# Loading later batches in the order of the attention's chunks, and copying v's global rows in two parts

## The chip, the cores and the metric

One core of a Trainium2 chip. The program runs on this core alone. The metric is the device time of one execution in microseconds (us); lower is better. The kernel before: 201.15 us, median of 3 runs (200.98 to 203.73).

A run is called slow if it took over 1.5% more than the fastest run of the same kernel, and comparisons use the other, fast, runs. Where two kernels are compared, a ratio is the mean time of the one's fast runs over that of the other's of the same rounds, so it is not quite the ratio of the medians quoted beside it.

## The reference

A sparse attention is followed by a gated long convolution. With 4 batches, 8 heads, 768 positions and 64 dimensions:

```python
keep = is_global | is_local      # the first 8 keys, and the last 96 up to the query
scores = where(keep, scale * q @ k.T + bias, -1e9)
a = exp(scores - max); a = a / (sum(a) + 1e-9)
x = (a @ v) as [batch, seq, 512]
x1, x2, x3 = split(x @ w_proj)                   # w_proj 512 x 1536
y = x1 * irfft(rfft(x2) * rfft(filter)) * x3     # along the sequence
out = y @ w_out
```

What matters here: every query attends to the first 8 keys. The kernel therefore keeps v in 7 tiles of 128 partitions: 120 rows of the sequence each, and in partitions 0 to 7 of **every** tile the same 8 global rows.

## The kernel before: the parts concerned

The kernel lists its operations with what they read and write; a scheduler written in it orders them for each engine. `load` issues a DMA from GpSimd ("G", casting float32 to float16) or SyncE ("S"):

```python
def load_rows(self, what, dst, src, b, t):        # 120 rows of k or v into one tile
    lo, hi = self.K0[t], self.K0[t] + KL
    self.load("G", dst[P - (hi - lo):P, t, :, 0:self.D], ...)

def load_v(self, b, ts):                          # [cut: reading vt, s]
    if b == 1:
        self.g.op("V", 0.2, lambda _: memset(vt[:, :, :, self.D:], 1.0), w=[("vn1", s)], ...)
    for t in ts:
        self.load_rows(("vn", s), vt, self.v, b, t)
        if t == 0:
            self.load_global(vt, s)

def load_global(self, vt, s):                     # the global rows: one copy, SBUF to SBUF
    self.load("S", vt[0:NG], vt[NG:2 * NG, 0:1].to_broadcast([NG, 7, self.H, self.D + 1]),
              [("vng", s)], (56, 1040), "vglobal", r=[("vn", s, 0), ("vn1", s)])

def load_batch(self, b):                          # batches 1 to 3
    for t in range(6):
        self.load_q(b, t)
    for t in range(7):
        self.load_rows(("kn",), self.kn, self.k, b, t)
    self.load_v(b, range(7))
```

Tile 0 of v is loaded from row 0 on, so its partitions 8 to 15 hold the global rows; the copy spreads them to partitions 0 to 7 of all tiles. The attention of a batch goes in three chunks, of tiles (0,1), (2,3) and (4,5,6). A chunk's values wait for the copy:

```python
def values(self, hp, c, slot):                    # head pair hp, chunk c
    def run(_):  # [cut] for each head and tile: E of the tile times v of the tile (L743),
                 # then E's overlap times v of the tile before (L748)
    vs = [("vn", slot, t) for t in range(max(0, ts[0] - 1), ts[-1] + 1)] + [("vn1", slot), ("vng", slot)]
    g.op("P", 0.03 * n, run, acq=[b], r=es + vs, name="values")
```

The first batch has a loader of its own, already by thirds, with its loads in the order q, k, v of a chunk.

The softmax here doesn't subtract the row's maximum and nothing guards it: scores larger than these inputs give would overflow.

Of the kernel before, what the change touches and what calls it, by code (L numbers as in the profile page):

```python
# [17 lines left out]
NG = 8  # L18
# [12 lines left out]
def dve(n, rate=1, psum=False):  # L31
    return 0.068 + (0.005 if psum else 0.0) + n / rate / 960.0
# [250 lines left out]
class Fused:  # L283
# [124 lines left out]

    def load_v(self, b, ts):
        vt, s = self.vn[b % 2], b % 2  # L410
        if b == 1:
            self.g.op("V", 0.2, lambda _: self.nc.vector.memset(vt[:, :, :, self.D:], 1.0),
                      w=[("vn1", s)], name="ones")
        for t in ts:
            self.load_rows(("vn", s), vt, self.v, b, t)
            if t == 0:
                self.load_global(vt, s)

    def load_global(self, vt, s):
        self.load("S", vt[0:NG], vt[NG:2 * NG, 0:1].to_broadcast([NG, 7, self.H, self.D + 1]),  # L420
                  [("vng", s)], (56, 1040), "vglobal", r=[("vn", s, 0), ("vn1", s)])

    def load_w(self, o, n):
        wr = self.w_proj.rearrange("(t p) n -> p t n", p=P)
# [302 lines left out]
    def values(self, hp, c, slot):  # L727
        nc, g, D = self.nc, self.g, self.D
        ts = self.GRP[c]
        nt = len(ts)  # L730
        b = g.bank()
        vt, xn = self.vn[slot], self.xn[hp]

        def view():
            return b.f32()[:, 0:2 * nt * (D + 1)].rearrange("p (h t d) -> p h t d", h=2, t=nt)

        def run(_):
            o, first = view(), True
            for hh in range(2):
                ef = self.E[hp][:, hh]  # L740
                for i, t in enumerate(ts):
                    at = 248 * t if t < 6 else 248 * 5 + 168
                    nc.tensor.matmul(o[:, hh, i], ef[:, at:at + P], vt[:, t, 2 * hp + hh, :],  # L743
                                     start=first, stop=(t == 0), skip_group_check=True)
                    first = False
                    if t > 0:
                        at = 248 * (t - 1) + KL
                        nc.tensor.matmul(o[:, hh, i], ef[:, at:at + P],  # L748
                                         vt[:, t - 1, 2 * hp + hh, :], start=False, stop=True,
                                         skip_group_check=True)  # L750
        n = 2 * sum(2 if t else 1 for t in ts)
        es = [("E", hp, i, hh) for i in range(max(0, c - 1), c + 1) for hh in range(2)]
        vs = [("vn", slot, t) for t in range(max(0, ts[0] - 1), ts[-1] + 1)] + [("vn1", slot), ("vng", slot)]
        g.op("P", 0.03 * n, run, acq=[b], r=es + vs, name="values")
        rc = self.rc[self.turn % 4]
        key = ("rc", self.turn % 4)
        self.turn += 1

        def scaled(_):
            o = view()  # L760
            r = rc[:, 0:2 * nt].rearrange("p (h t o) -> p h t o", h=2, o=1)
            nc.vector.reciprocal(r, o[:, :, :, D:D + 1])  # L762
            nc.vector.tensor_mul(xn[:, ts[0]:ts[0] + nt].rearrange("p t h d -> p h t d"),  # L763
                                 o[:, :, :, 0:D], r.to_broadcast([P, 2, nt, D]))
        g.op("V", 0.16 + 0.04 * nt + dve(2 * nt * D, 1, True), scaled, use=[b], w=[("xn", hp, c), key], name="xn")
# [214 lines left out]
                  [("g", 1, j, s) for j in range(4) for s in range(2)], (768, 2048), "filter")  # L980

    def load_batch(self, b):
        for t in range(6):
            self.load_q(b, t)
        for t in range(7):
            self.load_rows(("kn",), self.kn, self.k, b, t)
        self.load_v(b, range(7))

    def graph(self):
        g = self.g  # L990
# [61 lines left out]
```

## Time and profile before

| | before, the profiled run |
|---|---|
| time of that run / span in the profile | 199.61 us / 197.6 us |
| TensorE busy | 185.8 us, 94% |
| TensorE's waits for the copy | 2.0 us (batch 0), 1.9 us (batch 1) |
| mean granted clock of TensorE | 0.991 |

The span is from the first to the last instruction that the profiler saw; a run's time is some 2 us longer. The granted clock is TensorE's share of full speed. A mean of 0.991 over 197.6 us is 1.8 us of lost clock: one drop to half speed for 3.4 us (54.41 to 57.83 us at 0.50). The lines themselves are in the prediction.

### The profile page before, as it was taken

The numbers are of one execution on the slowest core, as the hardware profiler recorded it, in microseconds if no ns is written. First come the engines' busy times: TensorE is split into PE (matmuls) and PEld (weight loads), VectorE is DVE, ScalarE is ACT, GpSimd is POOL, SyncE is SP. The second block draws the span as 40 slices with busy tenths as digits, with TensorE's granted clock in tenths as the row PEclk, the third lists the DMA queues.
The fourth block names the chain that finished last, engine by engine and source line by source line (L and its number), as shares of the span: only waits on it lengthen the run. The fifth ranks groups of instructions, "written<-read, shape, count | busy, mean of one in ns | idle before, by whom it ended". The sixth has DMA issues, their size and how long they took to land.

```text
span 197.6 us, 4679 instructions
## 1 busy us (share of the span) xinstructions
PE 185.8 (94%) x1758; PEld 109.9 (56%) x1758; DVE 151.2 (77%) x383; ACT 155.6 (79%) x337; POOL 75.7 (38%) x96
## 2 busy tenths in 40 slices
PE   7965999999699999999999999999999999999992
PEld 2545767665435467665456756754556675445540
DVE  7795974997749999995099998994598999259630
ACT  7777995969868989994799979865897975785842
POOL 8799972799968918992000500000000000000000
PEclk9999999999969999999999999999999999999999
DMA  6999999999999999999700560005200000214025
GB/s 143 195 164 146 160 202 193 155 151 132 146 157 141 135 101 62 139 138 159 277 2 3 37 41 2 3 2 211 111 0 0 3 0 6 103 53 159 2 109 209
DMA packets 90885, 20.52 MB, mean 104 GB/s; under 512 B 83728, under 2 KB 87792, under 8 KB 90864
## 3 DMA queue, kind: packets, MB, share of 16 engines
q0 software_dynamic: 80912, 12.14, 101.8%
q1 hardware_dynamic: 9952, 8.10, 12.8%
q8 instruction: 13, 0.21, 0.5%
q14 instruction: 8, 0.07, 0.1%
HBM read 25.82 MB, written 6.29 MB: 163 GB/s over the span
## 4 chain that ended last, share of the span: by engine, by line
PE 77%; POOL 6%; DVE 5%; DMA 4%; ACT 3%; issue 2%; POOLq 0%; ACTq 0%; DVEq 0%
PE bank L805 21%; PE bank L852 11%; PE bank L892 10%; PE bank L872 8%; PE bank L645 7%; PE bank L694 5%; PE bank L743 3%; PE bank L778 3%; PE bank L658 3%; DMA vn<-vn 3%; POOL kn L383 3%; PE bank L748 2%; DMA kn<-in_k_dram 2%; POOL vn L383 2%; PE bank L685 2%
## 5 line engine op out<-in xcount | busy, mean ns | idle before, releaser
L709 ACT ACTIVATE E<-bank 128x432 f16<-128x432 f32 x96 | 43.7, 555 | 3.1 <-PE bank L694 2.9
L805 PE MATMUL bank<-xT,w 128*128 128x384 f16 x256 | 44.6, 326 | 0.5 <-DVE xT L367 0.3
L383 POOL DMA_DIRECT2D kn<-in_k_dram x28 | 26.2, 943 | 31.8 <-PE bank L645 18.7
L805 PEld LDWEIGHTS <-w 128*128 128x128 f16 x256 | 24.7, 98 | 17.3 <-issue 1.2
L383 POOL DMA_DIRECT2D vn<-in_v_dram x28 | 25.3, 916 | 0.9 <-DVE qn L367 0.9
L763 DVE TENSOR_TENSOR xn<-bank,rc 128x256 f16<-128x256 f32 (+1 forms) x48 | 22.5, 468 | 1.7
L371 ACT ACTIVATE ot<-bank 128x512 f32<-128x512 f32 x24 | 14.3, 597 | 10.8 <-PE bank L892 10.8
L892 PE MATMUL bank<-wo,y 128*128 128x512 f16 x96 | 22.4, 379 | 0.0
L743 PE MATMUL bank<-vn,E 128*128 128x65 f16 x224 | 17.5, 194 | 4.1 <-DMA kn<-in_k_dram 2.0
L813 DVE TENSOR_TENSOR g<-bank,x 128x384 f16<-128x384 f32 x32 | 17.3, 551 | 4.9 <-PE bank L805 4.5
L743 PEld LDWEIGHTS <-E 128*128 128x128 f16 x224 | 15.1, 98 | 8.8 <-DVE E L722 2.7
L371 ACT ACTIVATE x<-bank 128x384 f16<-128x384 f32 x27 | 13.4, 504 | 7.9 <-PE bank L805 6.5
L645 PE MATMUL bank<-ab,fwd 128*128 128x512 f16 x72 | 18.6, 379 | 0.0
L872 PE MATMUL bank<-inv,X 128*128 128x384 f16 x96 | 18.4, 326 | 0.1
L383 POOL DMA_DIRECT2D qn<-in_q_dram x18 | 16.1, 910 | 3.6 <-PE bank L694 1.7
L748 PE MATMUL bank<-vn,E 128*128 128x65 f16 x192 | 17.1, 194 | 0.0
L367 ACT CAST X<-bank 128x512 f16<-128x512 f32 x23 | 13.8, 603 | 3.0 <-PE bank L645 2.4
L367 ACT CAST eo<-bank 128x384 f16<-128x384 f32 x30 | 14.5, 507 | 2.0 <-PE bank L872 1.7
L762 DVE RECIPROCAL rc<-bank 128x4 f32<-128x4 f32 (+1 forms) x48 | 8.6, 178 | 9.3 <-PE bank L748 4.8
L694 PE MATMUL bank<-QT,KT 64*128 64x216 f16 (+2 forms) x224 | 15.4, 245 | 0.3 <-ACT E L709 0.2
L367 ACT CAST ab<-bank 128x512 f16<-128x512 f32 x20 | 11.9, 607 | 4.4 <-PE bank L852 4.4
L892 PEld LDWEIGHTS <-y 128*128 128x128 f16 x96 | 9.4, 98 | 10.6
(112 smaller groups left out, 344.9 us busy)
## 6 DMA issues: line engine op xcount, KB each, us to landing
out_dram<-ot SPq DMA_DIRECT2D x24, 256.0 KB, 2.0
kn<-in_k_dram POOLq DMA_DIRECT2D x28, 120.0 KB, 5.6
vn<-in_v_dram POOLq DMA_DIRECT2D x28, 120.0 KB, 6.7
qn<-in_q_dram POOLq DMA_DIRECT2D x18, 128.0 KB, 7.9
ot<-in_q_dram SPq DMA_DIRECT2D x6, 256.0 KB, 6.9
w<-in_moe_w_proj_dram POOLq DMA_DIRECT2D x4, 256.0 KB, 7.0
g<-in_moe_filter_fft_dram POOLq DMA_DIRECT2D x1, 768.0 KB, 12.8
w<-in_moe_w_proj_dram POOLq DMA_DIRECT2D x1, 512.0 KB, 9.7
```

What stands on the lines that cost most here:

```text
L367: {"A": nc.scalar.copy, "V": nc.vector.tensor_copy, "G": nc.gpsimd.tensor_copy}[e](out, in_)
L371: self.nc.scalar.mul(out, in_, c)
L383: return self.g.op(eng, 0.57 + 0.00035 * nbytes[0] if eng == "G" else 0.5, lambda _: e.dma_start(dst, src), w=w, r=r, nbytes=nbytes, name= ...
L645: self.nc.tensor.matmul(b.f32(), self.fwd[:, kt, s, :], src[i][:, kt, :], start=(kt == 0), stop=(kt == 2))
L694: nc.tensor.matmul(bs[hh].f32()[:, off:off + w], self.KT[hs, hp, P * m:P * m + P], self.QT[hs, hp, KL * m:KL * m + w], start=(off == 0 and ...
L709: g.op("A", act(432), lambda _, hh=hh: nc.scalar.activation(eo[:, hh], bs[hh].f32()[:, 0:432].rearrange("p (m w) -> p m w", m=2), Act.Exp, ...
L743: nc.tensor.matmul(o[:, hh, i], ef[:, at:at + P], vt[:, t, 2 * hp + hh, :], start=first, stop=(t == 0), skip_group_check=True)
L763: nc.vector.tensor_mul(xn[:, ts[0]:ts[0] + nt].rearrange("p t h d -> p h t d"), o[:, :, :, 0:D], r.to_broadcast([P, 2, nt, D]))
L805: nc.tensor.matmul(bk.f32()[:, 0:h], self.w[:, c, o + P * j:o + P * j + P], self.xT[:, c, h * s:h * s + h], start=(c == 0), stop=(c == 3))
L852: nc.tensor.matmul(bk.f32(), src[:, c, P * t:P * t + P], w[:, c, DM:2 * DM], start=(c == 0), stop=(c == 3))
L872: nc.tensor.matmul(bk.f32()[:, 0:h], X[:, s, cs], self.inv[:, s, :], start=(s == slots[0]), stop=(s == slots[-1]))
L892: nc.tensor.matmul(bk.f32(), y[:, c, P * t:P * t + P], self.wo[:, c, :], start=(c == 0), stop=(c == 3))
```

## The change

Two ideas. **Order**: for a batch after the first, the loads go by thirds (q, k and v of chunk 0, then of chunk 1, and so on), so tile 0 of v comes sixth instead of fourteenth and the copy can go sooner. **Split**: the copy goes in two parts, for tiles 0 and 1 (all that chunk 0 needs) and for the other five.

```diff
     def load_v(self, b, ts):
-        if b == 1:
+        if b == 1 and ts[0] == 0:
...
     def load_global(self, vt, s):
-        self.load("S", vt[0:NG], vt[NG:2 * NG, 0:1].to_broadcast([NG, 7, self.H, self.D + 1]),
-                  [("vng", s)], (56, 1040), "vglobal", r=[("vn", s, 0), ("vn1", s)])
+        for c, (t, n) in enumerate(((0, 2), (2, 5))):
+            self.load("S", vt[0:NG, t:t + n], vt[NG:2 * NG, 0:1].to_broadcast(
+                [NG, n, self.H, self.D + 1]), [("vng", s, c)], (8 * n, 1040), "vglobal",
+                r=[("vn", s, 0), ("vn1", s)])
...
-        vs = [("vn", slot, t) for t in range(max(0, ts[0] - 1), ts[-1] + 1)] + [("vn1", slot), ("vng", slot)]
+        vs = [("vn", slot, t) for t in range(max(0, ts[0] - 1), ts[-1] + 1)] + [("vn1", slot)] + [
+            ("vng", slot, i) for i in range(max(0, c - 1), min(c, 1) + 1)]
...
     def load_batch(self, b):
-        for t in range(6):
-            self.load_q(b, t)
-        for t in range(7):
-            self.load_rows(("kn",), self.kn, self.k, b, t)
-        self.load_v(b, range(7))
+        for c in range(3):
+            for t in ([0, 1, 2], [3, 4], [5])[c]:
+                self.load_q(b, t)
+            for t in self.GRP[c]:
+                self.load_rows(("kn",), self.kn, self.k, b, t)
+            self.load_v(b, self.GRP[c])
```

A comparison of the two built programs: TensorE, VectorE and ScalarE keep their sequence, except for one idle ("filler") matmul more on TensorE. GpSimd's order changes for batch 1 alone, since the scheduler had brought batches 2 and 3 to thirds already. SyncE has four copies more.

## The prediction

> **What bounds the kernel now.** I read the page's shares first, then TensorE's own waits, then the chain that ended last, then GpSimd's timeline around the one wait that the chain shows to be a DMA, and last a table of short windows.
>
> ```profile
> PE 185.8 (94%) x1758; PEld 109.9 (56%) x1758; DVE 151.2 (77%) x383; ACT 155.6 (79%) x337; POOL 75.7 (38%) x96
> ...
> PEclk9999999999969999999999999999999999999999
> DMA  6999999999999999999700560005200000214025
> ```
>
> TensorE is busy 94% of 197.6 us, so all that moving loads about can win is in the 11.8 us of its idle time and in the one slice where its clock digit drops to 6. The DMA row is full until about 100 us and nearly empty later: a change of load order can matter only in the first half.
>
> ```profile
> PE bank L743 <- DMA kn<-in_k_dram: 2.0, 1, 2.0
> PE bank L743 <- DMA vn<-vn: 1.9, 1, 1.9
> PE bank L658 <- DVE qn L367: 1.6, 1, 1.6
> ```
>
> These are TensorE's three longest waits in its own list. Line 743 is the first matmul of the attention's values. It happens twice: at 18.14 us (batch 0) and at 53.31 us (batch 1). Batches 2 and 3 have no such wait.
>
> The first is put down to a load of k, and I don't believe that. The matmul waits on two semaphores: that of the copy of the global rows of v, and that of v's tile 0. In the trace's semaphore records, the k load that the list names lands at 18.21 us or later, after the matmul has started; tile 0 of v had landed by 12.36 us; the copy's semaphore is complete at 18.0 us. So both waits are for the same thing, the copy vn<-vn that spreads 8 rows of tile 0 to all seven tiles.
>
> ```profile
> 46.25 0.86 PE bank L852 x4
> 47.11 0.35 PE bank L519 x6
> 47.46 0.02 issue
> 47.48 0.14 DVE inv L367
> 47.62 5.55 DMA vn<-vn
> 53.18 0.14 issue
> 53.31 0.22 PE bank L743 x2
> ```
>
> In the chain (start, us, what) the batch-1 copy takes 5.55 us from issue to landing, and TensorE is idle for the last 1.92 us of it. It is issued only at 47.62 us because tile 0 of v is the 14th of the batch's 20 loads:
>
> ```profile
> 31.27 0.94 POOL L383 DMA_DIRECT2D kn<-in_k_dram  x1 [1.37 <-DMA w<-in_moe_w_proj_dram]
> 35.09 0.92 POOL L383 DMA_DIRECT2D kn<-in_k_dram  x1 [2.89 <-DMA g<-in_moe_filter_fft_dram]
> 36.28 2.83 POOL L383 DMA_DIRECT2D kn<-in_k_dram  x3 [0.27 <-issue]
> 39.90 1.79 POOL L383 DMA_DIRECT2D kn<-in_k_dram  x2 [0.79 <-PE bank L805]
> 41.68 6.27 POOL L383 DMA_DIRECT2D vn<-in_v_dram  x7
> ```
>
> The seven v loads begin at 41.68 us, and the first lands 5.9 us later (47.56).
>
> ```profile
> 51.40:53.30 1.90, 0.00 (x0) 0.02 (x1) 0.99 (x3) 1.90 (x5) 1.49 (x2) 1.00 1.76 147
> 54.40:57.80 3.40, 3.40 (x23) 1.23 (x21) 1.52 (x6) 1.88 (x4) 1.72 (x3) 0.50 2.26 161
> ```
>
> The windows table (busy PE, PEld, DVE, ACT, POOL, then clock) shows the second cost of that wait: after 1.9 us without a matmul the next 3.4 us run at a clock of 0.50.
>
> [...]The 2.0 us gap at 16.1 to 18.1 us was not followed by a drop.
>
> [...]56 packets of 1040 bytes and 8 late semaphore steps for each copy. The split keeps the 8 partitions, [...]with 2 or 5 rows each instead of 7.
>
> [...]in the first copy (issued 12.44) an engine's seven rows start 0.07 us apart[...], but the engines' first rows start anywhere from 15.29 to about 16.7 us.
>
> **The change part by part.**
>
> *Order of loads.* The program order tells that TensorE, VectorE and ScalarE keep their sequences, banks included, but for one filler matmul. On GpSimd only batch 1 changes; in batches 2 and 3 the order was already q, k, v by thirds, as buffers come free that way. In batch 1 tile 0 of v moves from 14th to 6th.
>
> When is it issued? Each GpSimd load waits for the load eight places earlier, whose semaphore it takes over. q0 to q2 keep 22.84 to 25.86 us. k0 then follows the second weight load (landed 25.77), k1 the third (27.15), v0 the fourth (28.48), v1 the fifth (30.98). Next comes q3, behind the filter (34.80). So v0 is issued at about 28.5 instead of 41.68 us. Seven loads are outstanding behind the filter in either kernel when it lands, and v0 is the sixth of them: it lands where q5 landed, at about 40.0 us. The copy follows at once, and even at the old 5.55 us it is in place by 45.6 us, nearly 6 us before it is wanted at 51.4. What pays for it is q3, q4, k2 and k3: they land at about 41.8 to 44.3 us, and are wanted at 49.6 and 50.8. So nothing new should wait.
>
> How much of the 1.92 us comes back? The masked E of head pairs 0 and 1 is done by VectorE at about 51.0 and 51.5 us, that of pair 2 at 52.4, with one 0.65 us transform between. So the first values can start at about 51.4, and 1.8 of the 1.92 us is won.
>
> *The clock drop.* 3.41 us at half speed cost 0.5 x 3.41 = 1.7 us wherever TensorE is the bound, and in 54.6 to 57.8 it is: VectorE waits 1.81 us and ScalarE 1.40 us for it. In the profiled run this would also go. [...]I take half: 0.85 us.
>
> *Passing it on.* From 59.4 us VectorE is full and carries the chain. It idled 1.30 + 1.81 + 0.82 = 3.9 us between 52.4 and 59.4, all for TensorE, so it can start up to that much earlier. I let 95% through. After 86 us TensorE is at 100% and the shift is carried to the end.
>
> *Copy in two parts.* Five rows fewer in each engine at 0.07 us are 0.35 us off the first part, out of 5.55[...]. So at batch 0 I expect the wait to fall from 2.04 to about 1.7 us only. The added filler (about 0.22 us at the idle matmul's spacing) stands between pairs 2 and 3 of these very values and takes most of that back. Net 0.1 us. The four added issues are on SyncE, which idles; the 5-row part lands well before chunk 1 asks for it (22.2 us).
>
> Sum: 1.8 + 0.85 + 0.1 = 2.75, times 0.95 = 2.6 us; I add 0.2[...]: 2.8 us. 201.15 - 2.8 = about 198.3 us.
>
> **The rivals.**
>
> *The wait is replaced.* If the values were really held by E or by a bank, removing the copy would show a VectorE or ScalarE wait in its place and win under 1 us: about 200.5. Against it: ScalarE was busy through the gap, but on later work, and VectorE's masks for pairs 0 and 1 were finished by 51.54.
>
> *The loads that were pushed back hold TensorE.* q3, q4, k2 and k3 have 6 to 8 us in hand by the estimate above. If GpSimd were held longer behind the filter, TensorE would wait at line 658 instead, and the time would be 200 to 202. The filter landed at 34.8 us and 11 loads at 0.9 us follow; I see no room for that.
>
> *The split wins all of the batch-0 wait as well.* If queueing behind casting loads scales with rows[...], the first part takes 5.55 x 2/7 plus some 2 us and the wait of 2.04 goes. Then 2 us more are won, and with a clock drop avoided in some runs the time is 195.5 to 196.5. The packets of 0.07 us in bursts speak against it, though the batch-1 copy shows rows taking 0.14 us on average.
>
> *Nothing reaches the end*, because VectorE's stretch from 60 to 85 us absorbs it: about 200.5. Its idle time before 59.4 us speaks against it.
>
> **Range and chances.** The central case has 1.8 us sure and 0 to 1.7 us from the clock: 197.5 to 199.3. Rival three[...] reach down to 196.3, the first two up to 200.2. Faster by over 2% needs 4.0 us, which needs the clock drop in every run before and a piece of the third rival: 0.17. Slower has no cause that I can see but the filler and DMA luck: 0.02.
>
> **What would show it.** In TensorE's waits after: the 1.9 us on vn<-vn is gone; the 2.0 us at line 743's first matmul (line 745 now), whatever load it is put down to, is still 1.4 to 2 us. GpSimd issues v0 of batch 1 at 28 to 30 us and its copy goes out at about 40. The clock is 1.00 from 50 to 60 us. The values of batch 1 start at about 51.3, and the gate matmuls that began at 69.10 begin 2 to 3.5 us earlier. A wait for qn or kn at line 660 near 49 us, or a batch-0 wait under 1 us, would prove me wrong.

## The result, and the profile after

The changed kernel: **195.93 us** median (194.91 to 198.54, 4 runs); before, in the same rounds, 201.06 (200.55 to 203.73, 4 runs). Ratio of fast runs 0.9741, 95% interval 0.9685 to 0.9796: faster by 2.6%. The prediction of 198.3 us was 2.4 us too high, and the result lies just below its range, which began at 196.3.

The profile taken with this result fell in the slowest of the four runs (198.54 us). Its clock row and its longest wait on TensorE (columns: what waits, its releaser, then us in total, times, longest us):

```profile
PEclk9999699999999999999999999999999999999999
```

```profile
PE bank L745 <- DMA vn<-vn: 1.8, 1, 1.8
```

The drop in this run is at 20 us, in batch 0, and the only copy that TensorE still waits for is batch 0's. For a comparison with the profile of before I use a later profile of the same changed kernel (e4 below: 195.5 us, span 194.0 us), a fast run. Its page: shares, clock and DMA.

```profile
PE 184.9 (95%) x1759; PEld 109.8 (57%) x1759; DVE 150.7 (78%) x383; ACT 155.0 (80%) x337; POOL 76.0 (39%) x96
...
PEclk9999999999999999999999999999999999999999
DMA  6999999999999999999500900015100001114035
```

TensorE is busy 0.9 us less than before on one matmul more; nothing ran at half clock. TensorE's waits of the same run:

```profile
PE bank L745 <- DMA kn<-in_k_dram: 1.6, 1, 1.6
PE bank L660 <- DVE qn L367: 1.5, 1, 1.5
PE bank L363 <- DVE idle L434: 1.2, 1, 1.2
```

One wait at the first values is left, that of batch 0 (again put down to a load of k; the semaphore records show the copy). Next come lines of GpSimd's timeline and of TensorE's (start, us, engine, line, operation, count), then the two windows in which before had 0.00 us of matmul and a clock of 0.50 (start:end, length, then busy PE, PEld, DVE, ACT, POOL, each with its count, then clock, DMA share and GB/s):

```profile
28.32 0.90 POOL L383 DMA_DIRECT2D vn<-in_v_dram  x1
```

```profile
50.92 0.61 PE L660 MATMUL bank<-ident,kn 128*128 128x128 f16 x8
51.47 0.22 PE L745 MATMUL bank<-vn,E 128*128 128x65 f16 x2
```

```profile
51.40:53.30 1.90, 1.82 (x26) 1.17 (x24) 1.83 (x7) 1.90 (x6) 1.90 (x3) 1.00 1.62 147
54.40:57.80 3.40, 3.40 (x28) 1.24 (x26) 2.58 (x7) 3.40 (x9) 2.14 (x3) 1.00 2.28 159
```

v's tile 0 of batch 1 is issued at 28.32 us (before: 41.68), the copy goes out at 41.67 and lands at 47.27, and the values start at 51.47 us straight behind the transposes. The clock holds at 1.00.

### The profile page after: what moved, and what is told of

It is laid out like the page before. It is cut to its first block, busy times and chain, and to the rows that moved or that the text cites.

```text
span 197.0 us, 4691 instructions
## 1 busy us (share of the span) xinstructions
PE 186.6 (95%) x1759; PEld 110.9 (56%) x1759; DVE 150.7 (76%) x383; ACT 155.2 (79%) x337; POOL 76.3 (39%) x96
## 4 chain that ended last, share of the span: by engine, by line
PE 80%; DVE 8%; ACT 5%; DMA 3%; issue 2%; ACTq 0%; DVEq 0%
PE bank L808 21%; PE bank L895 11%; PE bank L855 10%; PE bank L875 8%; PE bank L647 7%; PE bank L696 5%; PE bank L363 4%; PE bank L745 3%; PE bank L781 3%; PE bank L660 3%; DMA vn<-vn 3%; PE bank L750 2%; PE bank L687 2%; ACT E L711 2%; DVE QT L367 1%
## 5 line engine op out<-in xcount | busy, mean ns | idle before, releaser
L745 PE MATMUL bank<-vn,E 128*128 128x65 f16 x224 | 17.9, 195 | 2.0 <-DMA vn<-vn 1.8
L745 PEld LDWEIGHTS <-E 128*128 128x128 f16 x224 | 15.4, 98 | 7.0 <-DMA kn<-in_k_dram 1.9
L750 PE MATMUL bank<-vn,E 128*128 128x65 f16 x192 | 17.4, 194 | 0.0
L367 ACT CAST X<-bank 128x512 f16<-128x512 f32 x23 | 13.7, 609 | 2.1 <-PE bank L647 1.5
L750 PEld LDWEIGHTS <-E 128*128 128x128 f16 x192 | 13.8, 98 | 1.2
```

Source lines behind the costliest of these rows:

```text
L367: {"A": nc.scalar.copy, "V": nc.vector.tensor_copy, "G": nc.gpsimd.tensor_copy}[e](out, in_)
L745: nc.tensor.matmul(o[:, hh, i], ef[:, at:at + P], vt[:, t, 2 * hp + hh, :], start=first, stop=(t == 0), skip_group_check=True)
L750: nc.tensor.matmul(o[:, hh, i], ef[:, at:at + P], vt[:, t - 1, 2 * hp + hh, :], start=False, stop=True, skip_group_check=True)
```

## The experiments

Twelve runs in four calls; the kernels of a call ran on the same chip and share eleven runs of before.

| run | median us | before's median | ratio of fast runs, 95% | fast runs |
|---|---|---|---|---|
| e1 before, again | 201.69 | 200.64 | 1.0076 [1.0008, 1.0144] | 6 of 6 |
| e2 order only | 196.71 | 200.64 | 0.9855 [0.9788, 0.9921] | 6 of 6 |
| e3 split only | 199.69 | 200.64 | 0.9996 [0.9938, 1.0054] | 6 of 6 |
| e4 after, again | 195.69 | 200.64 | 0.9805 [0.9735, 0.9875] | 6 of 6 |
| e5 before + warm batch 1 | 200.25 | 201.34 | 0.9958 [0.9889, 1.0028] | 5 of 6 |
| e6 before + warm batches 0, 1 | 200.46 | 201.34 | 0.9967 [0.9903, 1.0031] | 5 of 6 |
| e7 after + warm batch 0 | 196.02 | 201.34 | 0.9757 [0.9710, 0.9805] | 6 of 6 |
| e8 after, ones sooner | 197.20 | 201.34 | 0.9720 [0.9649, 0.9792] | 3 of 6 |
| e9 only tile 0 of v moved | 197.43 | 201.66 | 0.9851 [0.9768, 0.9933] | 5 of 6 |
| e10 staged global rows | 195.27 | 201.66 | 0.9743 [0.9681, 0.9805] | 6 of 6 |
| e11 after, third time | 197.72 | 202.34 | 0.9721 [0.9645, 0.9797] | 3 of 6 |
| e12 staged, again | 195.25 | 202.34 | 0.9690 [0.9637, 0.9742] | 6 of 6 |

My theory after the result: the order of loads does it all, by taking batch 1's wait away *and* by a clock drop that the wait brings about in nearly every run of before. The rival: the split (the copy in two parts) does much of it, at batch 0 or by making the copy quicker. A second rival: the clock drop, not the wait, is most of it.

### e1: the kernel before, unchanged

No edit.

> The kernel before, unchanged, to see the granted clock of each of its runs, which the times of before alone do not list. Theory A (the gain was larger than forecast because the clock drop behind the 1.9 us wait happens in nearly every run of before, and a second one at the batch-0 gap in many): most runs have a mean clock of 0.991 or 0.982, none 1.000, and the time follows the clock by about 1.5 us per drop. Theory B (the clock is not what I mis-sized; the split or the order saves waits that I called small): about half the runs at 1.000, and those are near 199 us. Ratio to before 1.000 within 0.3% in either case.

It came out 0.8% *slower* than itself on the same chip, with an interval that leaves out 1: differences below about 1% are not safe here, whatever their interval. Part of it comes from the rule for slow runs: it left out four runs of before of 201.4 to 202.5 us, while five of e1's, of 201.3 to 202.1 us, count as fast, since e1's fastest run is slower. Its profile (span 200.1 us) shows what the first profile of before did not: a longer wait for the copy, and a second clock drop, in batch 0. Waits, chain and windows:

```profile
PE bank L743 <- DMA kn<-in_k_dram: 2.6, 1, 2.6
PE bank L743 <- DMA vn<-vn: 1.9, 1, 1.9
```

```profile
47.92 8.26 DMA vn<-vn
56.18 0.14 issue
56.31 0.22 PE bank L743 x2
```

```profile
16.26:19.67 3.41, 0.74 (x12) 0.43 (x10) 1.16 (x3) 3.38 (x12) 3.41 (x5) 1.00 2.61 147
19.67:23.09 3.42, 3.42 (x48) 2.80 (x46) 2.24 (x8) 0.91 (x2) 2.59 (x5) 0.50 2.17 151
53.81:57.22 3.41, 1.47 (x24) 1.07 (x23) 2.05 (x6) 2.76 (x7) 2.59 (x3) 1.00 1.76 174
57.22:60.63 3.41, 3.41 (x22) 1.28 (x21) 1.44 (x6) 1.51 (x4) 1.83 (x3) 0.50 2.39 153
```

The copy took 8.26 us here, against 5.55 in the first profile. (The wait reads 1.9 us in both, for TensorE itself came to it later; how long the whole stretch was is in the table below.) In both pairs of windows, 3.41 us with TensorE busy 0.74 or 1.47 us are followed by 3.4 us at 0.50.

### e2: the order alone

```diff
 (after, with load_global and the values' list of the kernel before)
```

> Batch 1's loads by thirds, the copy in one piece. Every engine but the load queue has the program of the kernel before. Theory A: this is nearly the whole gain, 195.5 to 197 us, TensorE's batch-1 wait on the copy gone, the batch-0 wait of about 2 us still there. Theory B (the split matters): 198 to 199 us, and the split gives the other 2 to 3 us. As forecast, it should be 198.3.

196.71 us, 1.5% faster than before. Its waits on TensorE, in which batch 1's is gone:

```profile
PE bank L743 <- DMA vn<-vn: 1.9, 1, 1.9
PE bank L658 <- DVE qn L367: 1.6, 1, 1.6
```

The order alone brings the larger part. The whole change (e4) is 0.5% below it, with overlapping intervals.

### e3: the split alone

```diff
 (before, with load_global and the values' list of the change; load_batch stays)
```

> The copy in two parts, loads in the old order, and the one added filler matmul. Theory A: 200 to 201 us, within 0.3% of before: the batch-0 wait 1.7 us or more, the batch-1 wait 1.5 us or more. Theory B: 197.5 to 199 us, with a batch-0 wait under 1 us.

0.9996: nothing to be seen. TensorE still waits for the copy in batch 1, for 2.9 us. Its first part there, of 2 rows to a partition, took 7.17 us. The chain:

```profile
47.08 7.17 DMA vn<-vn
54.25 0.14 issue
54.39 0.22 PE bank L745 x2
```

So the rival that the copy's time goes with its rows falls: over six profiles each, batch 0's copy took 4.73 to 5.90 us whole (mean 5.63) and 4.37 to 5.82 as a first part (mean 5.33). In the profile of after, the first parts issued at 13.86 and 41.43 us took 5.64 and 5.74 us (DMA share 2.85 and 2.53), and the one at 74.54 us, beside less traffic (0.89), 3.04 us.

### e4: the changed kernel again

No edit against after.

> The changed kernel again, to have a profile of a run in the fast state and the clocks of more runs. Both theories: 195 to 197 us. Theory A: runs at 1.000 are near 195, those at 0.991 near 196.5. In the profile TensorE's wait for the copy at batch 1 is gone; the batch-0 wait is 1.5 to 2 us.

195.69 us, 2.0% faster; profile above.

### e5 and e6: before, with the clock kept up

If the clock drop is most of the gain, idle matmuls ahead of the values, which do nothing else, should win it without any load moved.

```diff
+    WARM = {'first1': 8}            # e6: {'first0': 6, 'first1': 8}
     def fill(self, out):
+            if o.eng == "P" and o.name in self.WARM:     # 8 idle matmuls into the bank
+                ... d.fn = lambda _: self.busy(8, b)      # of the operation that follows
```

> The kernel before plus 8 idle matmuls (about 1.7 us of work for nobody) ahead of batch 1's first values, in the bank that these values use next; nothing else moves. They keep TensorE's clock up while the wait for the copy stays as it is. Theory A (each drop of the clock costs about 1.5 us, and before loses two in most runs): the drop near 54 to 58 us is gone, at most one is left, mean clock 0.990 or better, and the time is 1.0 to 1.7 us under before although useless work was added. Rival (the clock drop lies beside other work and costs nothing, the wait itself is the whole gain): same as before within 0.2%.

> The same with 6 more idle matmuls ahead of batch 0's first values. Theory A: no drop left in most runs, clock 1.000, 2 to 3 us under before (about 198), so that what still separates it from the changed kernel, 2 to 2.5 us, is the wait for the copy alone. Rival: same as before; or slower, if the idle matmuls outlast the wait of 2 to 2.6 us.

The drop behind batch 1's wait is gone from both profiles, but the time fell by only 0.4% and 0.3%, with intervals that contain 1: not the 1.0 to 1.7 and 2 to 3 us that theory A had expected. Here is e5's timeline of TensorE at the wait:

```profile
51.83 1.89 PE L371 MATMUL bank<-idle 128*128 128x512 f16 x8
55.70 0.22 PE L751 MATMUL bank<-vn,E 128*128 128x65 f16 x2 [1.99 <-DMA qn<-in_q_dram]
```

In this run the copy landed at 55.56 us, over 2 us later than in the first profile of before (53.18), so TensorE stood idle for 1.99 us even after the fillers. The drop was avoided all the same (clock 1.00 from 51.53 to 58.35 us). The second rival falls as the main cause: the clock alone gives 0.4% where the change gives 2% to 3%. How much of the clock's share late copies hid here is open. The runs' clocks say more than the profile: five runs of e5 and e6 have a clock of 0.995 or more, and a mean span of 198.0 us. That is no drop before the end: e6's profile, at 0.995, has one in its last 2 us alone. The four fast runs of before with about one drop, on the same chip, have 197.9.

### e7: after, with the clock kept up in batch 0

```diff
+    WARM = {'first0': 6}            # on top of after; fill() as in e5
```

> The changed kernel plus the 6 idle matmuls ahead of batch 0's first values, where it still waits 1.6 us and in some runs drops its clock. Theory A: every run at a clock of 0.999 to 1.000, times close together at 194.9 to 195.5 us, 0.3 to 0.8 us under the changed kernel's mean. Rival: no gain, for a drop at 20 us falls into a stretch where ScalarE is the bound.

196.02 us, as after (its fast runs' mean is 195.97, e4's 195.99); the six runs lie between 195.30 and 196.39. The gain that theory A expected did not come. Five of its runs are without a drop (0.995 or more), with a mean span of 194.3 us: 3.7 less than the five of e5 and e6 without one, on the same chip.

### e8: after, with batch 0's tile 0 of v sooner

The first load of v waits for a memset of the ones column; here that comes first on VectorE.

```diff
-                  w=[("vn1", 0)], name="ones", bias=-3000)
+                  w=[("vn1", 0)], name="ones", bias=-4600)
```

> The changed kernel with the memset of v's column of ones moved to the front of VectorE's program, for the load of batch 0's tile 0 of v stands 0.9 us behind it on GpSimd. That load, its copy and every later load of the first stretch come 0.9 us sooner. If the batch-0 wait is for the copy, it falls from 1.6 to about 0.7 us and the time by 0.7 to 1.0 us, to about 194.6; if it only uncovers another wait there (a k load, or the exponentials), by under 0.3 us.

Three fast runs with a mean of 195.23 us, and three of 198.6 to 199.5: inconclusive. The profile (span 193.2 us) has batch 0's values at 17.2 us, about 0.9 sooner. The wait before them is still 1.4 us, and though it is put down to E, the copy lands at 17.06, as close before the values as in before (18.00 and 18.14).

### e9: only tile 0 of v moved

Is it the thirds, or just the copy's source? Before, with one load of batch 1 (and its copy) taken from fourteenth to sixth.

```diff
+        for t in range(3):
+            self.load_q(b, t)
+        for t in range(2):
+            self.load_rows(("kn",), self.kn, self.k, b, t)
+        self.load_v(b, [0])
+        # then q 3 to 5, k 2 to 6, v 1 to 6
```

> The kernel before with a single load moved: batch 1's tile 0 of v goes from 14th to 6th place, behind k1; its copy stays in one piece, q, k and the other v tiles keep their old order among themselves, and batches 2 and 3 are untouched. If the order matters only through the time at which tile 0 lands and its copy goes out, this gives all that the order by thirds gave: TensorE's batch-1 wait gone, first values of batch 1 about 24.3 us after the first gate matmuls of batch 0, 196 to 197 us. Rival (the later v tiles or k2, k3 matter as well): a part of it is missing, 198 to 199 us, and TensorE waits for another load.

0.9851, as e2's 0.9855. GpSimd's timeline and the longest waits:

```profile
28.24 0.90 POOL L383 DMA_DIRECT2D vn<-in_v_dram  x1
...
42.75 5.38 POOL L383 DMA_DIRECT2D vn<-in_v_dram  x6
```

```profile
PE bank L658 <- DMA kn<-in_k_dram: 2.1, 4, 0.7
PE bank L743 <- DMA vn<-vn: 1.2, 1, 1.2
```

The four waits for k lie before 17 us, in batch 0, and the 1.2 us end at 18.24 us, which is batch 0 as well. Batch 1's wait is gone, though the other six v loads go out as late as before. When the copy's source is loaded is the cause; the thirds as such add nothing that can be told.

### e10: batch 0's global rows without a copy

An attempt at a version that beats both: batch 0's eight rows are loaded a second time as float32 on SyncE, behind q2, and ScalarE or VectorE casts and spreads them to tiles 0 and 1.

```diff
+        self.gs = t("gs", [NG, H, D], F32)
+            if c == 0:
+                self.load("S", self.gs, self.v[0, :, 0:NG, :].rearrange("h p d -> p h d"), ["gs"], ...)
+        if b == 0:   # instead of the copy's first part
+            self.g.op("AV", ..., lambda e: self.copy(e, vt[0:NG, 0:2, :, 0:self.D],
+                self.gs[:, None].to_broadcast([NG, 2, self.H, self.D])), r=["gs"], w=[("vng", 0, 0)])
```

> An attempt at a better version: the changed kernel, with the global rows of batch 0's tiles 0 and 1 loaded on their own as f32 (8 partitions, 16 KB in all) at the start and spread with a cast by ScalarE, so that batch 0's first values no longer wait for a copy that waits for a load. The scheduler orders the first stretch anew. If the batch-0 wait of 1.6 us is the copy's, first values of batch 0 come at about 16 to 16.5 us instead of 18.1, no clock drop at 17 to 20 us, and the time is 193.3 to 194.5 us. If exponentials, k loads or the weights hold the stretch anyway, 195 to 196.5, as the changed kernel.

195.27 us. The wait for the copy is gone and batch 0's values start at 16.50 us, but the gate matmuls after them start no sooner (see e12).

### e11 and e12: after and the staged version, side by side

> The changed kernel once more, beside the staged version on one chip and in the same rounds. 195 to 197 us, ratio to before 0.974 to 0.981 as in the two sets so far; clock 1.000 in about half of the runs, 0.991 in the rest, never below 0.986.

> The staged version again. If it is better than the changed kernel: 194.3 to 196 us, under the changed kernel's mean of the same rounds by 0.5 to 1.5 us, most of it because fewer runs have a late start of batch 0. Rival: the difference of 0.5 us in the medians was chance, and the two are the same within 0.2%.

In these rounds after had three fast runs (194.65, 196.61, 196.75) and three slow ones (198.7 to 200.9); the staged version was 194.46 to 196.45 in all six, as in e10. In e12 the values of batch 0 start at 15.04 us, three sooner than in before, yet the gate matmuls after them at 27.24 us as in e4 (27.23). Probably ScalarE holds them, busy 7.00 of 7.00 us (the fourth busy column) as in the same window of e4, but TensorE is busy 6.66 us too, and no run tests it:

```profile
20.00:27.00 7.00, 6.66 (x123) 5.08 (x118) 5.01 (x19) 7.00 (x22) 6.40 (x8) 1.00 1.56 173
```

Batch 1's values come 0.8 us sooner than in e4 (50.69 against 51.47). The fast means are 195.16 and 195.34 us, against 195.99 and 196.0 for the change: 0.3 to 0.4% lower, which is under the 1% that e1 calls for. No slow runs showed: 12 of 12 fast, against after's 12 of 16.

## Why the prediction was wrong

**The stretches.** The profiles give the time from the first gate matmuls of batch 0 to batch 1's first values (which holds the wait), and from there to the gate matmuls of batch 1 (which holds the drop). All in us; the profiles of after and e11 are slow runs, but these stretches of them are as in the fast ones:

| profile | to batch 1's values | on to its gates | sum |
|---|---|---|---|
| before; e1; e3 (old order, drop) | 26.3; 26.3; 27.3 | 15.0; 14.8; 15.1 | 41.3; 41.1; 42.4 |
| e5; e6 (old order, kept warm) | 28.2; 26.9 | 13.2; 13.2 | 41.4; 40.1 |
| e2; after; e4; e7; e8; e9; e11 (tile 0 early) | 24.4; 24.2; 24.2; 24.3; 24.4; 24.2; 24.5 | 13.6; 13.5; 13.6; 13.5; 13.7; 13.5; 13.8 | 37.7 to 38.3 |
| e10; e12 (tile 0 early, staged) | 23.5; 23.5 | 13.7; 13.5 | 37.2; 36.9 |

From batch 1's gates to the end it is about 129 us in all of those that I compared (before 129.3, e2 129.0, e4 128.9): what is won there reaches the end.

**The runs.** All fast runs of before (34 of 50) and of after (12 of 16), with the granted clock that each run records. A clock of 0.991 is one drop, 0.983 two:

| | before | after |
|---|---|---|
| mean time, us | 200.86 | 195.89 |
| of it in the span / outside | 198.84 / 2.02 | 194.33 / 1.57 |
| without a drop: runs, mean span | 0 | 6, 193.65 |
| about one drop: runs, mean span | 13, 197.82 | 6, 195.00 |
| two: runs, mean span | 21, 199.47 | 0 |

Sorted like this, the 4.96 us between the two fall into: 2.82 at equal drops (197.82 - 195.00); 1.7 for drops, from 1.62 to 0.5 in a run at about 1.5 us each (195.00 - 193.65 = 1.35 and 199.47 - 197.82 = 1.65); and 0.45 outside the span.

This is a sorting of runs on several chips and not an experiment. In the profiles the one drop of before lies in batch 1 and that of after in batch 0, so equal counts are not like with like. And the one experiment on the drop shows less: e5 took about one drop from each run and its fast runs won 0.8 us (199.96 against 200.75, an interval that reaches zero), while without a drop on either side, on one chip, 3.7 us of span remain (e5 and e6 against e7, which has the split too). By these two readings the wait's share is 2.8 or 3.7 us and the drops' 1.7 or 0.8; the runs do not settle which.

By the prediction's own steps:

- *The place and the mechanism*: right. Batch 1's wait for the copy is gone, v0 was issued at 28.32 us (forecast 28.5), the values began at 51.47 (forecast 51.3 to 51.4), no wait at line 660 near 49 us took its place, and neither rival with a replaced wait came about. The gate matmuls of batch 1 came 3.2 us sooner (68.29 to 65.09; forecast 2 to 3.5; the 69.10 in the prediction is a later one of them). The copy went out at 41.67 us (forecast 40) with 4 us in hand.
- *"1.8 of the 1.92 us is won"*: the step that failed, a term of the sum that was mis-sized. The five profiles in the old order need 26.3 to 28.2 us for the first stretch and those with tile 0 early 24.2 to 24.5: between the means, 27.0 and 24.3, lie 2.7 us, and single profiles of the old order lose 2.0 to 3.9: before and e1 2.0, e3 3.0, and e6 and e5, which also hold the idle matmuls, 2.6 and 3.9. The run statistics say 2.8 to 3.7 (above). I had read one profile, whose copy (5.55 us) was the quickest of the five in the old order; the others took 6.66 to 8.26.
- *"I take half: 0.85 us"*: the reasoning failed. That only about half of the runs would pay for the gap was my estimate, and no trace showed it. None of the 50 runs of before whose clocks are on record, fast or slow, was without a drop (the highest clock is 0.991), and with tile 0 early none of the nine profiles has one behind batch 1's values. The second stretch is 1.4 to 1.5 us shorter (15.0 against 13.5), nearly the 1.7 that I had worked out and then halved. But e5 won only 0.8 us in all, so how far 0.85 was too small stays open.
- *Copy in two parts, 0.1 us net*: not contradicted. The first part is 0.3 us quicker (forecast 0.35), e3 shows no gain, e4 against e2 0.5% at most. The rival that had the split win all of batch 0's wait is refuted by e3 and by the 1.6 us (e4, fast), 1.8 and 2.4 us (after and e11, slow) still waited there.
- *"times 0.95"*: held as far as it can be told; from batch 1's gates on the difference is kept.
- *The starting point*: I subtracted a saving read from a profiled run of 199.61 us from a median of 201.15. The slower runs have a drop more (0.983, mean span 199.47 us, against 197.82) and, in e1's profile, a longer copy (8.26 us against 5.55), so they have more to win. From that profile to e4's the full terms happen to hold: 197.6 - 194.0 = 3.6 us, against 1.8 + 1.7 + 0.1.
- *"Faster by over 2% ... needs the clock drop in every run before and a piece of the third rival"*: a drop was in every run before; the piece of the third rival wasn't needed.

**What stays open.** The parts of wait and clock are not cleanly apart: late copies can both lengthen the wait and bring the drop (in e1 the copy took 8.26 us and 3.4 us at 0.50 followed), and e5 and e6, which take the drop away by itself, won only 0.3 to 0.4%, though their second stretch is 1.8 us shorter; the sums of both stretches differ by some 0.8 us (41.6 with a drop, 40.75 without, means of three and two profiles). Nor do I know why 0.45 us fall outside the span: the time less the span is 1.5 to 1.7 us in all 28 runs of after, e3, e4, e7 and e11, and 1.7 or more in every run of the others, e8 and the staged version, which also have the split, among them. If every run of before has batch 1's drop, as its three profiles do (before, e1, e3), then the drop in batch 0 comes in about 6 of 10 fast runs before and, by the six of twelve, about half of those after: the change hardly bears on it.

## What to carry to other kernels

When several operations wait for a small copy, look first at when its *source* is loaded: moving one load eight places forward (e9, 0.9851) did what splitting the copy (e3, 0.9996) could not. Read a saving from several profiles, or set it beside each run's clock, before you trust its size: a profile of a fast run can show a shorter wait and fewer drops than most runs have. And a wait can cost again after it ends: in the 3.41 us before four of the drops (one in before, two in e1, one in after) TensorE was busy for 0.74 to 1.54 us (22 to 45%), and the next 3.4 us ran at 0.50. Not every such wait did: before's batch 0 had 1.36 us busy in the 3.41 us up to 18.16 us, and the clock stayed at 1.00. So look in the recorded clocks how many runs have the drop, and test what it is worth, for here the experiment showed less than the sorted runs.
